# A gated delta-rule layer with a feed-forward block: a stated order of steps from the third chunk on, h W2 as seven products of blocks, K^T and Q^T in buffers of their own

## The chip, the cores and the metric

One core of one Trainium2 chip. The metric is the device time of one execution in microseconds (us); lower is better. TensorE (PE) multiplies, VectorE (DVE) and ScalarE (ACT) work elementwise, GpSimd (POOL) does some of that too, SyncE (SP) issues DMA transfers; ACT and POOL can issue them as well. Each engine works through a queue of its own in order, and waits in it for the results of others.

## The reference, cut to what matters

```python
# q, k, v: (4, 8, 768, 48), beta: (4, 8, 768); fp32
k_n = k / (norm(k) + 1e-6)
state = zeros(B, H, D, D)
for t in range(S):
    y[:, :, t] = einsum('bhd,bhde->bhe', q[:, :, t], state)
    v_old = einsum('bhde,bhd->bhe', state, k_n[:, :, t])
    state = state + beta_t * einsum('bhd,bhe->bhde', k_n[:, :, t], v_t - v_old)
x = y.transpose(0, 2, 1, 3).reshape(B, S, 384)
xn = (x - mean(x)) / sqrt(var(x) + 1e-6) * g_ln
out = x + maximum(xn @ w_ch1, 0) @ w_ch2      # w_ch1 384x1536, w_ch2 1536x384
```

## The kernel before, in words

The 768 tokens are cut into 12 chunks of C = 64 tokens, for all 4 batches at once: 256 rows of x a chunk. Two chunks make a slab. For a chunk the token loop is replaced by matrix work:

- **Loads.** `load_blocks` (L168) fetches K and Q in 32x32 blocks, K from chunk 4 on by POOL's queue, Q by SP's; `load_k` (L184) and `load` fetch K by rows and V, by SP.
- **K^T and Q^T.** `turned` (L348) transposes the blocks on DVE into the two halves of one tile `kqt` (three buffers).
- **Gram and product.** `gram` (L368) makes K K^T on PE, ACT copies it to `gsb` (L376, L383). `product` (L393) makes K Q^T, DVE masks it into `pt` (L395).
- **The inverse.** A triangular matrix of each chunk and head has to be inverted. `blocks(m)` does the 32x32 diagonal blocks for a slab (two chunks) on DVE: it clears the block `xb` (POOL, L535), transposes the gram (L477), scales it (L546), takes 31 elimination steps of two instructions each (L555, L560), and transposes the result (L483, `own`), which goes to `xt` (L468, L472). `join` (L574 to L631) then fills the blocks off the diagonal with small matmuls `p_e` (L580) and `p_z` (L626). `first_blocks` and `first_join` are a form with 16x16 blocks, for the first two slabs.
- **Scaling of v.** `norms` takes the norm of k: squares on ACT (L411, L413), sums on DVE (L417), root on ACT (L419), plus 1e-6 on POOL (L420). `scale_v` (L428) multiplies v by it, on POOL from chunk 2 on.
- **The recurrence.** `recur(c)`: `p_k` and `p_y` from K^T, Q^T and the state (L652), v minus `p_k` (L657), `p_u` (L663), `p_s` (L675) and the state's update (L678), `p_y` with `pt` (L683), its copy to x (L688), the layer norm (L694 to L701), and the transpose of its result `p_n` (L709) to `xnt` (L710).
- **The feed-forward block.** `ffn(c)`: 12 tiles of h, each 3 matmuls `p_h` in the program (L724; each is two instructions on PE, as are all 128-row fp32 products here but the transposes) and a relu on ACT (L730); then for each half of the rows 12 matmuls with w_ch2 into `p_o` (L746), the residual add on DVE (L735) and the store by SP (L737).

The order of the work: the first part is written out by hand under `in_this_order`, which ties the instructions of each engine to their written order. From chunk 0's feed-forward block on, a `Plan` gives every step a due time (T = 45 units a chunk); the steps are emitted by due time, and the scheduler may still move instructions between them. The recurrence of chunk c is due beside the feed-forward block of chunk c - 1, in some places beside its end; the grams and the inverse of the next slab are spread over the two chunks before it. `behind_each` keeps the joins behind the latest feed-forward matmul.

PSUM tiles have four tags: `att` (two buffers: p_e, p_z, p_n), `two` (one: p_g, p_k, p_u, p_s), `by` (one: p_y), `ffn` (two: p_h, p_o).

Of the kernel before, what the change touches and what calls it, by code (L numbers as in the profile page):

```python
# [67 lines left out]
@contextmanager  # L68
def behind(tc, last):

    with ExitStack() as stack:
        for ins in last.values():
            stack.enter_context(tc.issue_after(ins))
        yield


def behind_each(tc, last, gen):

    while True:
        with behind(tc, dict(last)):  # L80
            try:
                next(gen)
            except StopIteration:
                return
        yield
# [8 lines left out]
def kernel(  # L94
# [101 lines left out]

    def load_turned(c):
        load_blocks(k, c, 0, (nc.gpsimd,))
        load_blocks(q, c, 1, (nc.sync,))
# [146 lines left out]
    def turned(c, n):  # L346

        nc.vector.transpose(  # L348
            made[c][0][:, :, n].rearrange("p i (u t) -> p i u t", t=32), tblocks[(2 * c + n) % NTB]
        )  # L350

# [5 lines left out]
    def gram(c, fine=False, maker=ps_two):  # L357

        kqt = made[c][0]
        p_g = ps_g(maker)  # L360
        for j in range(GP):
            for u in range(2) if fine else (0,):
                for hp, e in TILES:
                    rows = slice(DP * hp, DP * hp + D)
                    i = e * GP + j
                    r0 = BK * u
                    out_ = p_g[C * e + r0 : C * e + r0 + (BK if fine else C), hp, j, 0 : C - r0]
                    nc.tensor.matmul(  # L368
                        out_, kqt[rows, i, 0, r0 : r0 + (BK if fine else C)], kqt[rows, i, 0, r0:C]
                    )  # L370
        dst = grams[c].rearrange("p (j n) t -> p n j t", n=2)
        if fine:
            nc.scalar.copy(dst[:, :, :, 0:BK], p_g[:, :, :, 0:BK])
            yield
        else:
            nc.scalar.copy(dst, p_g)  # L376
        for e in range(2):
            if fine:
                rows = slice(C * e, C * e + BK)
                nc.scalar.copy(dst[rows, :, :, BK:C], p_g[rows, :, :, BK:C])  # L380
            else:
                rows = slice(C * e + BK, C * e + C)
                nc.scalar.copy(dst[rows, :, :, 0:BK], p_g[rows, :, :, BK:C])  # L383

    def product(c):

        kqt = made[c][0]
        p_g = ps_g()
        for j in range(GP):
            for hp, e in TILES:  # L390
                rows = slice(DP * hp, DP * hp + D)
                i = e * GP + j
                nc.tensor.matmul(p_g[half(e ^ hp), hp, j], kqt[rows, i, 0], kqt[rows, i, 1])  # L393
        pt = work.tile([128, GH, C], FP32, name="pt", bufs=3)
        nc.vector.tensor_tensor(  # L395
            out=pt.rearrange("p (j n) t -> p n j t", n=2), in0=p_g,
            in1=pmask[:, None, None, :].to_broadcast([128, 2, GP, C]), op=ALU.mult,
        )
        made[c].append(pt)
# [4 lines left out]
    def norm_parts(c, scratch=None):  # L404
# [15 lines left out]
        nc.gpsimd.tensor_scalar_add(knrm, knrm, 1e-6)  # L420
# [6 lines left out]
    def scale_v(c, knrm, eng):  # L427
        eng.tensor_tensor(  # L428
            out=vs[c], in0=vs[c], in1=knrm[:, :, None].to_broadcast([128, GH, D]), op=ALU.mult
        )  # L430

    def new_chunk(c):
        if c % SLAB == 0:
            pairs[c // SLAB] = work.tile([128, SLAB, GH, C], FP32, name="gsb", bufs=2)
        grams[c] = pairs[c // SLAB][:, c % SLAB]
        made[c] = [work.tile([128, GH, 2, C], FP32, name="kqt", bufs=3)]

    def prep_v(c):
        if c > 2:
            load_kv(c)  # L440
        yield
        scale_v(c, norms(c), nc.gpsimd)
        yield

    def prep_g(c, fine=False):

        new_chunk(c)
        turned(c, 0)
# [5 lines left out]
    def prep_p(c):  # L454

        turned(c, 1)
# [5 lines left out]
    N_BLOCKS = 3 + BK // 2  # L462
# [11 lines left out]
    def blocks(m):  # L474
# [6 lines left out]
        def scatter(xb):  # L481
            own = blk.tile([128, SLAB * GH, BK], FP32, name="own", tag="gb")
            nc.vector.transpose(own.rearrange("p h t -> p t h"), xb[:, 0].rearrange("p s t -> p t s"))  # L483
            for i in range(SLAB):
# [39 lines left out]
    def inverse(nb, L, beta_l, gather, scatter):  # L524
# [10 lines left out]
        nc.gpsimd.memset(xb, 0.0)  # L535
        gb = square(both, 1) if L == FB else square(blk.tile([128, BK * BK], FP32, name="gb"), 0)
        gather(gb)
        yield
        nrm = blk.tile([128, BK], FP32, name="nrm")[:, 0 : nb * L].rearrange("p (b s) -> p b s", b=nb)
        nc.scalar.sqrt(nrm, diagonal(gb))  # L540
        nc.vector.tensor_scalar_add(nrm, nrm, 1e-6)
# [24 lines left out]
    N_JOIN = 2  # L566

    def join(chunks, both=()):

        last = None  # L570
        for c in chunks:
            xt, gsb = xts[c % NXT], grams.pop(c)
            xn = swapped("x_n").rearrange("p (h t) -> p h t", t=BK)
            nc.vector.transpose(xn, xt[:, :, 0:BK])  # L574
# [60 lines left out]
    N_RECUR = 6  # L635

    def recur(c):

        kqt, pt = made.pop(c)
        kp, xt, vv = kraws[c % NK], xts[c % NXT], vs[c]  # L640
# [5 lines left out]
        if c:  # L646
            p_k = ps(ps_two, "p_k")
            for n, dst in ((0, p_k), (1, p_y)):
                for j in range(GP):
                    for hp, e in TILES:  # L650
                        rows = slice(DP * hp, DP * hp + D)
                        nc.tensor.matmul(  # L652
                            dst[half(e), hp, j], kqt[rows, e * GP + j, n], s_all[rows, e, j],
# [43 lines left out]
        nc.scalar.activation(rstd, mv[:, :, 1], ACTF.Sqrt, bias=eps)  # L697
        nc.vector.reciprocal(rstd, rstd)
# [15 lines left out]
    N_FFN = FT + 2 * FT // 2  # L714

    mlp = {}

    def ffn(c):
        xnt, x = xnts.pop(c), xs.pop(c)
        hs = []  # L720
        for f in range(FT):
# [6 lines left out]
            mlp["PE"] = nc.cur_bb.bb.instructions[-1]  # L728
            h_f = work.tile([128, TOK], FP32, name="h_f", bufs=FT)
            nc.scalar.activation(h_f, p_h, ACTF.Relu)  # L730
            hs.append(h_f)
            yield
        def store(g, p_o):
            o = work.tile([128, DM], FP32, name="o", bufs=2)
            nc.vector.tensor_tensor(out=o, in0=p_o, in1=x[:, g], op=ALU.add)  # L735
            for e in range(2):
                nc.sync.dma_start(  # L737
                    out=out[2 * e + g, c * C : (c + 1) * C, :], in_=o[e * C : (e + 1) * C]
                )


        for gs in ((0, 1),) if c == 0 else ((0,), (1,)):
            p_os = [ps_ffn([128, DM], "p_o") for g in gs]
            for f in range(FT):
                for g, p_o in zip(gs, p_os):
                    nc.tensor.matmul(  # L746
                        p_o, hs[f][:, g * 128 : (g + 1) * 128], w2_sb[:, f],
                        start=(f == 0), stop=(f == FT - 1),
                    )
                mlp["PE"] = nc.cur_bb.bb.instructions[-1]  # L750
                if f % 2 and f < FT - 1:
                    yield
            for g, p_o in zip(gs, p_os):
                store(g, p_o)
            yield
# [9 lines left out]
    with in_this_order(tc) as last:  # L765
# [25 lines left out]
        scale_v(0, knrm, nc.vector)  # L791
# [5 lines left out]
        joining = join((0,), both=piece)  # L797
        next(joining)
# [22 lines left out]
        for _ in range(3):  # L821
# [6 lines left out]
    def second():  # L828
# [12 lines left out]
        scale_v(1, norms(1), nc.vector)  # L841
        yield

    def queries():
        for c in (2, 3):
            load_blocks(q, c, 1, (nc.sync,))
        load_kv(2)
        load_beta()

    T = 45  # L850
    starts = [0, 14, 64] + [80 + T * i for i in range(NCH - 2)]
    ends = [2, 26, 80] + starts[4:]
# [3 lines left out]

    plan.once(39, early.close)
    for c in range(NCH):
        t0, t1 = starts[c], ends[c]
        if c > 1:  # L860
            plan.spread(prep_v(c), 2, t0 - 72, t0 - 12)
        if c:
            plan.once(t0, begin, c)
        plan.spread(recur(c) if c else recur_0, N_RECUR if c else 1, t0, t1)
# [4 lines left out]
    plan.spread(ffn(1), N_FFN, 42, 80)  # L869
    for c in range(2, NCH):  # L870
        plan.spread(ffn(c), N_FFN, starts[c + 1], starts[c + 1] + T)
    for m in range(1, NSL):
        chunks = range(SLAB * m, SLAB * m + SLAB)
        t = starts[SLAB * m]
        if m > 1:

            times = (t - 70, t - 58, t - 18, t - 13) if m > 2 else (t - 56, t - 46, t - 18, t - 13)
            for i, c in enumerate(chunks):
                plan.once(times[0] - 15 + 5 * i, load_turned, c)
            plan.spread(in_turn(*(prep_g(c) for c in chunks)), SLAB * 2, times[0], times[1])  # L880
            plan.spread(blocks(m), N_BLOCKS, times[1], times[2])
            plan.spread(in_turn(*(prep_p(c) for c in chunks)), SLAB * 2, t - 25, t - 10)
        else:
            times = (16, 24, 44, 56)
            plan.spread(in_turn(*(prep_g(c, True) for c in chunks)), SLAB * 2, times[0], times[1])
            plan.spread(in_turn(*(prep_p(c) for c in chunks)), SLAB * 2, 30, 46)
            plan.once(10, queries)
            plan.spread(first_blocks(tuple(chunks)), 4 + FB // 2, times[1], times[2])

            def then(c):  # L890
                yield from first_join(c)
                to_xt(c)
                yield

            plan.spread(in_turn(*(then(c) for c in chunks)), 6, 44, times[3])
        joining = join(chunks)
        plan.spread(joining if m == 1 else behind_each(tc, mlp, joining), 3, times[3], t - 2)
    with behind(tc, after):
        plan.run()

# [29 lines left out]
```

## Time and profile before

| | |
|---|---|
| median of 4 runs | 617.01 us (609.12 to 619.4) |
| the profiled execution | 617.27 us, its span 615.4 us |
| PE busy | 541.2 us, 88% of the span |
| DVE busy | 322.6 us, 52% |
| ACT busy | 170.1 us, 28% |
| POOL busy | 80.5 us, 13% |
| granted TensorE clock, mean over the span | 0.971 |
| p_h matmuls (L724) | 206.7 us in 864 instructions |
| p_o matmuls (L746) | 201.5 us in 576 instructions |

The busy time of an engine is the time in which at least one of its instructions was at work; loads of weights into TensorE are counted apart (PEld) and run beside the matmuls. Matmuls overlap, so the mean duration of one is longer than the distance from one start to the next; the pace is read from starts in the timeline. A number in brackets in a timeline's line is the time that the engine had stood idle before it, and the instruction that ended that.

### The profile page before, as it was taken

The page shows a single profiled execution, that of the slowest core. Times are in us where ns is not written, and L with a number is a line of the kernel's source. Part 1 is how long each engine was busy: PE and PEld are TensorE (multiplying, and loading weights), DVE is VectorE, ACT ScalarE, POOL GpSimd, SP SyncE. Part 2 cuts the span into 40 slices and gives each one's busy share as a digit, 9 for nine tenths or more (in the row PEclk, how much of TensorE's full clock was granted, in tenths as well). Part 3 has the DMA queues.
Part 4 walks back from the last instruction along what each step waited for, and adds up shares of the span by engine and source line. Part 5 has one row for each costly group of instructions (what it writes and reads, how often), then busy time and mean ns, then how long its engine had stood idle before and what let it go on. Part 6 is the DMA issues. An engine that isn't in the chain of part 4 may idle for free.

```text
span 615.4 us, 20905 instructions
## 1 busy us (share of the span) xinstructions
PE 541.2 (88%) x9512; PEld 404.5 (66%) x9512; DVE 322.6 (52%) x681; ACT 170.1 (28%) x351; POOL 80.5 (13%) x128
## 2 busy tenths in 40 slices
PE   2036886987999959999999999999999999999997
PEld 2035665565767746866867867768758678677673
DVE  5835869993246993229964059952179720201000
ACT  1213252503333205241224232243322142122120
POOL 5000116331040202300302200011000010000000
PEclk9999879898999988999999999999999999999999
DMA  4716879526044600411610510200200000000101
GB/s 54 192 42 154 185 163 245 75 49 91 16 84 66 103 9 18 85 34 28 99 20 16 93 25 15 53 16 15 53 14 15 1 19 12 14 15 1 27 1 26
DMA packets 126919, 34.51 MB, mean 56 GB/s; under 512 B 121184, under 2 KB 124272, under 8 KB 126832
## 3 DMA queue, kind: packets, MB, share of 16 engines
q1 hardware_dynamic: 110256, 19.14, 18.8%
q0 software_dynamic: 3504, 10.25, 6.5%
q10 hardware_dynamic: 13072, 3.80, 2.7%
q8 instruction: 74, 1.21, 0.8%
q14 instruction: 13, 0.11, 0.1%
HBM read 28.44 MB, written 4.72 MB: 54 GB/s over the span
## 4 chain that ended last, share of the span: by engine, by line
PE 53%; DVE 27%; SPq 7%; issue 6%; DMA 3%; ACT 3%; ACTq 0%; DVEq 0%
PE p_o L746 20%; PE p_h L724 18%; DVE tmp L555 8%; DVE xb L560 8%; SPq L168 6%; PE p_g L368 2%; DMA tb<-in_k_dram 2%; PE p_e L580 2%; PE p_y L683 2%; PE p_z L626 2%; PE p_g L393 1%; DVE kqt L348 1%; DVE own L483 1%; SPq L184 1%; PE p_k L652 1%
## 5 line engine op out<-in xcount | busy, mean ns | idle before, releaser
L724 PE MATMUL p_h<-xnt,w_sb 128*128 128x256 f32 x864 | 206.7, 393 | 5.1 <-DVE o L735 4.4
L746 PE MATMUL p_o<-w_sb,h_f 128*128 128x384 f32 x576 | 201.5, 499 | 0.0
L724 PEld LDWEIGHTS p_h<-xnt,w_sb 128*128 128x128 f32 x864 | 164.4, 195 | 32.9 <-DVE o L735 4.0
L746 PEld LDWEIGHTS p_o<-w_sb,h_f 128*128 128x128 f32 x576 | 107.5, 193 | 65.8 <-issue 3.3
L730 ACT ACTIVATE h_f<-p_h 128x256 f32<-128x256 f32 x144 | 55.2, 383 | 192.6 <-PE p_h L724 192.5
L168 POOL DMA_DIRECT2D tb<-in_k_dram x64 | 42.5, 671 | 111.2 <-DVE tmp L555 57.4
L560 DVE TENSOR_TENSOR xb<-xb,tmp 128x31 f32<-128x31 f32 (+20 forms) x154 | 51.1, 332 | 5.1
L735 DVE TENSOR_TENSOR o<-p_o,x_ln 128x384 f32<-128x384 f32 x24 | 13.2, 549 | 74.0 <-PE p_o L746 74.0
L555 DVE TENSOR_TENSOR tmp<-xb,gb 128x31 f32<-128x31 f32 (+15 forms) x124 | 42.3, 341 | 3.8
L694 DVE BATCH_NORM_STATS2 st<-x_ln 128x6 f32<-128x384 f32 x24 | 12.3, 545 | 49.7 <-ACT x_ln L688 49.7
L678 DVE TENSOR_TENSOR s_all<-s_all,p_s 128x768 f32<-128x768 f32 x11 | 10.4, 941 | 47.2 <-PE p_s L675 47.1
L348 DVE STREAM_TRANSPOSE kqt<-tb 128x1024 f32<-128x1024 f32 x24 | 29.2, 1232 | 4.1 <-DMA tb<-in_k_dram 3.8
L368 PE MATMUL p_g<-kqt 48*64 48x64 f32 (+2 forms) x1024 | 16.9, 239 | 12.0 <-DVE kqt L348 8.1
L368 PEld LDWEIGHTS p_g<-kqt 48*32 48x32 f32 (+1 forms) x1024 | 14.8, 133 | 17.5 <-DVE kqt L348 8.3
L610 PE MATMUL p_e<-x_n,gsb 32*32 32x16 f32 x512 | 6.3, 189 | 22.4 <-DVE x_n L605 17.3
L420 POOL TENSOR_SCALAR knrm<-knrm 128x16 f32<-128x16 f32 x12 | 3.1, 256 | 163.9 <-ACT knrm L419 163.9
L417 DVE TENSOR_REDUCE ksum<-ksq 128x8 f32<-128x384 f32 x22 | 12.1, 550 | 21.2 <-ACT ksq L411 10.9
L580 PE MATMUL p_e<-x_n,gsb 32*32 32x32 f32 x768 | 16.1, 200 | 7.7 <-DVE mv L695 5.8
L580 PEld LDWEIGHTS p_e<-x_n,gsb 32*32 32x32 f32 x768 | 14.8, 113 | 11.0 <-DVE mv L695 6.0
L393 PEld LDWEIGHTS p_g<-kqt 48*64 48x64 f32 x768 | 14.0, 142 | 11.8 <-DVE s_all L678 6.5
L610 PEld LDWEIGHTS p_e<-x_n,gsb 32*32 32x32 f32 x512 | 5.7, 118 | 24.2 <-ACT xt L411 16.4
L657 DVE TENSOR_TENSOR v_raw<-v_raw,p_k 128x768 f32<-128x768 f32 x11 | 10.5, 952 | 20.8 <-PE p_k L652 20.8
(99 smaller groups left out, 521.1 us busy)
## 6 DMA issues: line engine op xcount, KB each, us to landing
words<-in_moe_w_ch_dram POOLq DMA_DIRECT2D x9, 768.0 KB, 5.6
out_dram<-o SPq DMA_DIRECT2D x48, 96.0 KB, 2.2
k<-in_k_dram SPq DMA_DIRECT2D x44, 96.0 KB, 3.1
v_raw<-in_v_dram SPq DMA_DIRECT2D x22, 192.0 KB, 4.3
tb<-in_q_dram SPq DMA_DIRECT2D x44, 64.0 KB
words<-in_moe_w_ch_dram ACTq DMA_DIRECT2D x3, 768.0 KB, 6.1
tb<-in_k_dram POOLq DMA_DIRECT2D x32, 64.0 KB, 2.8
tb<-in_q_dram SPq DMA_DIRECT2D x44, 32.0 KB, 2.2
```

What stands on the lines that cost most here:

```text
L168: engs[m % len(engs)].dma_start(out=dst[p0 : p0 + 32, :, u, 0:w], in_=src[:, hp::2, toks, 32 * m : 32 * m + w].rearrange("b j t d -> t (b ...
L348: nc.vector.transpose(made[c][0][:, :, n].rearrange("p i (u t) -> p i u t", t=32), tblocks[(2 * c + n) % NTB])
L368: nc.tensor.matmul(out_, kqt[rows, i, 0, r0 : r0 + (BK if fine else C)], kqt[rows, i, 0, r0:C])
L393: nc.tensor.matmul(p_g[half(e ^ hp), hp, j], kqt[rows, i, 0], kqt[rows, i, 1])
L555: nc.vector.tensor_tensor(out=t, in0=xb[:, :, 0:n, j : j + 1].to_broadcast([128, nb, n, w]), in1=gb[:, :, j : j + 1, j + 1 : L].to_broadca ...
L560: nc.vector.tensor_tensor(out=rest, in0=rest, in1=t, op=ALU.subtract)
L580: nc.tensor.matmul(p_e[r1, h], gsb[r0, h, BK:C], xn[r0, h])
L626: nc.tensor.matmul(p_z[r0, h], es[r1, h], xt[r1, h, BK:C])
L724: nc.tensor.matmul(p_h, w1_sb[:, t, f * 128 : (f + 1) * 128], xnt[:, t], start=(t == 0), stop=(t == KC - 1),)
L730: nc.scalar.activation(h_f, p_h, ACTF.Relu)
L735: nc.vector.tensor_tensor(out=o, in0=p_o, in1=x[:, g], op=ALU.add)
L746: nc.tensor.matmul(p_o, hs[f][:, g * 128 : (g + 1) * 128], w2_sb[:, f], start=(f == 0), stop=(f == FT - 1),)
```

## The change

**h W2 as seven products.** From chunk 1 on the product of h (256x1536) and w_ch2 (1536x384) is cut into 2x2 blocks: h into A11, A12, A21, A22 of 128x768, w_ch2 into blocks of 768x192. Instead of eight products of blocks there are seven, with sums of blocks (the Strassen-Winograd form): S1 to S4 are sums of blocks of h, made for each chunk on DVE (128x768 each; three of them in place); t2, t3, t4 are sums of blocks of w_ch2, made once on DVE (steps T), t1 takes the place of a block of w_ch2. P1 to P7 are the products, each six matmuls of 192 columns in the program, twelve instructions on PE. They add up in PSUM in three results, a, b and c; c and b are the two halves of one tile `p_o`. The steps d1 to d7 (eight instructions of 192 columns on DVE) read them and add them with x to the output.

**A stated order.** The plan ends with the joins of chunks 2 and 3. From chunk 2 on, `slot(c, order)` runs a string of steps, under `in_this_order` for all engines. A slot holds the recurrence of chunk c (KQ: L652 and v's subtraction; U; S; PU; L1 and L2: the layer norm; N: p_n), the feed-forward block of chunk c - 1 (H: one of twelve tiles of h with its relu; then S, P and d), the next chunks' transposes (TK, TQ), grams (G), products (PT, with the mask on DVE), and the inverse of the next slab (ga, no: gather and scale; r: two elimination steps; R: all that are left; own, xt, xn, J: the results and the joins). Vk and Vs: norms and scaling of v for chunk c + 1. An inverse is now done a slab ahead: its joins run in the odd slot before the slab that needs them. Slots 2 to 5 have strings of their own; slot 3 holds all elimination steps of the inverse for chunks 4 and 5.

**Smaller parts.** K^T and Q^T get tiles of their own (`kqt` becomes `kt` with 4 buffers and `qt` with 2). The loads for chunk c + 2 are issued right behind the transpose of chunk c, all by SP. Clearing `xb` goes from POOL to ACT for 32x32 blocks. The 1e-6 moves from POOL's L420 into `scale_v`, which is now always one DVE instruction. `load_kv(c + 2)` stands at the start of slot c; chunk 3's is fetched ahead of beta.

```diff
-        made[c] = [work.tile([128, GH, 2, C], FP32, name="kqt", bufs=3)]
+        made[c] = {}
...
+        made[c][n] = work.tile([128, GH, C], FP32, name="kq"[n] + "t", bufs=(4, 2)[n])
         nc.vector.transpose(
-            made[c][0][:, :, n].rearrange("p i (u t) -> p i u t", t=32), tblocks[(2 * c + n) % NTB]
+            made[c][n].rearrange("p i (u t) -> p i u t", t=32), tblocks[(2 * c + n) % NTB]
         )
+        if more and c + 2 < NCH:
+            load_blocks((k, q)[n], c + 2, n, (nc.sync,))
...
-        nc.gpsimd.tensor_scalar_add(knrm, knrm, 1e-6)
...
+        nc.vector.scalar_tensor_tensor(
+            out=vs[c], in0=knrm[:, :, None].to_broadcast([128, GH, D]), scalar=1e-6, in1=vs[c],
+            op0=ALU.add, op1=ALU.mult,
...
+            nc.scalar.mul(xb, eps[:, :, None, None].to_broadcast([128, nb, L, L]), 0.0)
...
+        t2, t3, t4 = (late.tile([128, HF, HM], FP32, name=f"t{i}") for i in (2, 3, 4))
+            for t, x0, x1 in ((t3, b22, b12), (b12, b12, b11), (t2, b22, b12), (t4, b21, t2)):
+                nc.vector.tensor_tensor(out=t, in0=x0, in1=x1, op=ALU.subtract)
+                yield
...
+    def mlp(c):
+        h, x = new_h(), xs.pop(c)
+        os = [work.tile([128, DM], FP32, name="o") for g in range(2)]
+        a11, a21, a12, a22 = (h[i][:, :, g * 128 : (g + 1) * 128] for i in range(2) for g in range(2))
+        s1, s2, s3, s4 = a21, a11, late_pool[0].tile([128, HF, 128], FP32, name="s3"), a12
...
+        def mul(n, a, b, first=False):
+            if n == "a" and first:
+                p["a"] = ps_ffn([128, HM], "p_a")
+            if n == "c" and "c" not in p:
+                p_cb = ps_ffn([128, DM], "p_o")
+                p.update(c=p_cb[:, 0:HM], b=p_cb[:, HM:])
+            for f in range(HF):
+                nc.tensor.matmul(
+                    p[n], a[:, f], b[:, f], start=(first and f == 0), stop=(f == HF - 1), skip_group_check=True,
+                )
...
+            "S3": lambda: add(s3, a11, a21, ALU.subtract),
+            "S1": lambda: add(s1, a21, a22),
+            "S2": lambda: add(s2, s1, a11, ALU.subtract),
+            "S4": lambda: add(s4, a12, s2, ALU.subtract),
+            "P1": lambda: mul("a", a11, w11, True),
+            "P2": lambda: mul("c", a12, w21, True),
+            "P5": lambda: mul("b", s1, t1),
+            "P6": lambda: mul("a", s2, t2),
+            "P3": lambda: mul("b", s4, w22),
+            "P7": lambda: mul("a", s3, t3),
+            "P4": lambda: mul("c", a22, t4, True),
+            "d1": lambda: add(o11, "a", x11),
+            "d2": lambda: add(o11, "c", o11),
+            "d5": lambda: add(o22, "b", x22),
+            "d6": lambda: add(o12, "a", x12),
+            "d3": lambda: (add(o12, "b", o12), store(c, 0, os[0])),
+            "d7": lambda: (add(o22, "a", o22), add(o21, "a", x21)),
+            "d4": lambda: (add(o21, "c", o21), store(c, 1, os[1])),
...
+    orders = {
+        2: """H H H KQ H H H T H T H T H T H U H S3 TK(a2) H P1 S1 d1 TK(b2) S2 S P2 d2 S4 PU P5 d5 L1
+            G(a2) P6 d6 L2 TQ(b) P3 d3 N G(b2) P7 d7 ga PT(b) P4 d4 no Vk Vs""",
+        3: """H r H KQ H r H r H r U TQ(a2) H r H r H r S H r PU H r H S3 H P1 S1 L1 d1 S2 PT(a2) L2
+            P2 d2 S4 r P5 d5 r P6 d6 TK(a4) N r P3 G(a4) d3 TK(b4) r P7 d7 G(b4) P4 d4 R own Vk Vs""",
+        4: """H H KQ xt' H xn' H H J' H H J' H U H J' H ga S H no S3 TQ(b) PU r H P1 L1 S1 PT(b) d1 S2
+            L2 P2 d2 S4 r P5 d5 r P6 d6 r N P3 d3 r P7 d7 r P4 d4 Vk Vs""",
+        5: """H r H KQ H r r H r H R U TQ(a2) H H own TK(a4) H S H H xt S3 PU H xn H L1 P1 S1 PT(a2) d1
+            S2 L2 P2 d2 S4 TK(b4) P5 d5 J P6 d6 G(a4) N P3 d3 J G(b4) P7 d7 J P4 d4 Vk Vs""",
+    }
+    even = """H H ga KQ no H r H r H r U H r H TQ(b) H r S H r H S3 PU r H H L1 P1 S1 PT(b) d1 S2 L2
+        P2 d2 S4 P5 d5 r P6 d6 r N P3 d3 r P7 d7 r P4 d4 Vk Vs"""
+    odd = """H r H r KQ H r H H R U TQ(a2) H H own TK(a4) H S H H xt S3 PU H xn H L1 P1 S1 PT(a2) d1 S2
+        L2 P2 d2 S4 TK(b4) P5 d5 J P6 d6 G(a4) N P3 d3 J G(b4) P7 d7 J P4 d4 Vk Vs"""
...
+    with in_this_order(tc):
+        for c in range(SLAB, NCH):
+            slot(c, orders.get(c, odd if c % SLAB else even))
+        steps = mlp(NCH - 1)
+        for name in "H H H H H H H H H S3 H H H P1 S1 d1 S2 P2 d2 S4 P5 d5 P6 d6 P3 d3 P7 d7 P4 d4".split():
+            steps[name]()
```

In the strings, a and b are the two chunks of the slot's slab, a2 and b2 those of the next, a4 and b4 of the one after; a prime marks a step for the slot's own slab.

## Prediction
> **What bounds the kernel now.** I read the page's first part, then its groups, then the table by stages, then the timeline.
>
> ```profile
> PE 541.2 (88%) x9512; PEld 404.5 (66%) x9512; DVE 322.6 (52%) x681; ACT 170.1 (28%) x351; POOL 80.5 (13%) x128
> L724 PE MATMUL p_h<-xnt,w_sb 128*128 128x256 f32 x864 | 206.7, 393 | 5.1 <-DVE o L735 4.4
> L746 PE MATMUL p_o<-w_sb,h_f 128*128 128x384 f32 x576 | 201.5, 499 | 0.0
> ```
> ```profile
> 247.00:334.00 87.00, 84.53 (x1404) 62.96 (x1404) 50.30 (x110) 26.35 (x55) 14.72 (x21) 1.00 0.27 47
> 334.00:421.00 87.00, 84.57 (x1404) 63.08 (x1404) 50.28 (x110) 26.35 (x55) 9.59 (x13) 1.00 0.20 38
> 421.00:508.00 87.00, 84.65 (x1406) 62.95 (x1404) 47.42 (x106) 24.68 (x51) 1.73 (x2) 1.00 0.09 20
> ```
>
> Columns of the second fence: window, length, busy time of PE, PE's weight loads, DVE, ACT and POOL (counts in brackets), then TensorE's clock, DMA share, GB/s. Each window is one pair of chunks. PE works 84.5 of 87 us at full clock; DVE 50. So from chunk 4 on TensorE is the bound, and only less TensorE work can gain much. The timeline says the same by start times:
>
> ```profile
> 246.88 1.15 PE L652 MATMUL p_k<-s_all,kqt 48*64 48x48 f32 x64
> ...
> 286.88 1.56 PE L724 MATMUL p_h<-xnt,w_sb 128*128 128x256 f32 x6 [0.93 <-DVE o L735]
> 288.37 1.15 PE L652 MATMUL p_k<-s_all,kqt 48*64 48x48 f32 x64
> ...
> 309.99 1.16 PE L393 MATMUL p_g<-kqt 48*64 48x64 f32 x64 [1.26 <-DVE s_all L678]
> ```
> ```profile
> 229.05 1.92 PE L580 MATMUL p_e<-x_n,gsb 32*32 32x32 f32 x64 [5.82 <-DVE mv L695]
> ```
>
> The next pair begins at 334.12, so a pair takes 87.24 us. The waits in brackets are all that PE loses in steady state; the 5.82 us (a join behind the inverse, once, for chunks 4 and 5) is the largest after 165 us.
>
> **Durations that I use.** From starts on PE:
>
> ```profile
> 281.26 0.82 PE L709 MATMUL p_n<-ident,xn_ln 128*128 128x128 f32 x6
> 281.91 2.75 PE L746 MATMUL p_o<-w_sb,h_f 128*128 128x384 f32 x8
> ...
> 571.93 7.91 PE L746 MATMUL p_o<-w_sb,h_f 128*128 128x384 f32 x24
> 579.67 15.70 PE L724 MATMUL p_h<-xnt,w_sb 128*128 128x256 f32 x72
> 595.21 15.64 PE L746 MATMUL p_o<-w_sb,h_f 128*128 128x384 f32 x48
> ```
>
> p_o: 24 in 7.74 us, 322.5 ns for 384 columns. p_h: 72 in 15.54, 215.8 ns for 256. The line through both is 2.5 ns + 0.833 ns a column. p_n: 6 in 0.65, 108 ns for 128 (line: 109).
>
> **The seven products.** h W2 is 48 instructions of 384 columns a chunk, 15.48 us. After, it is 7 x 6 x 2 = 84 of 192 columns. 192 columns do not occur before. Low end: the line, 162.5 ns, 13.65 us. High end: the weight load sets the pace, and the load groups of p_h and p_o show 195 and 193 ns, so 195 ns, 16.38 us. I take the line: p_n's load lasts 147 ns in its group, yet its matmuls start every 108, so a load's recorded length is not the time by which it holds the next matmul. That is -1.83 us a chunk, for 11 chunks (chunk 0 keeps the plain form) -20.1 us; at the high end +9.9.
>
> The Trainium skill ("TensorE: Matmul & The Clock Gate", section "Back-to-back issue gap") speaks against this edit: in a stream of weight load and matmul pairs the spacing is set by both, 81 ns at 128 columns where the column count alone gives 56. An estimate by that page, 25 ns more on each of 924 matmuls, would be +23 us, about 625 instead of the forecast below. The p_n row above shows no such excess at 128 columns, so the sum does without it.
>
> **What the products cost DVE.** By the rows 128x384 (0.549) and 128x1024 (L546, 1.23), 192 columns are 0.35 us and 768 are 0.95. A chunk gains S1 to S4 (3.8), eight output adds (2.8), loses two L735 (1.1), and takes v's scaling from POOL (L428, 1.475 there; 0.96 on DVE, as in its two early calls): +6.5. A pair goes from 50.3 to 63.3 us, under PE's 78 to 81. The four weight sums (1152 columns, 1.36 each) run once, in chunk 2's slot. On average all of it is hidden; in order it isn't, see below.
>
> **Moved and hidden.** K^T's eight loads a chunk go from POOL's queue to SP's, behind chunk c's transpose and ahead of later stores: 8 x 0.6 us (two L168 issue in 1.14) more in a queue that then issues for about 18 us in a 40 us slot, one or two slots early; uncovered, 5 us a slot. Clearing the inverse's block goes from POOL to ACT, a 128x1024 pass, 1.0 us by L376; ACT is busy 26 of 87 us; uncovered, 5 in all. POOL's knrm add goes; DVE waited for it only 8.0 us, early. Own buffers for K^T and Q^T remove a dependence on old products, worth nothing while loads are early. The inverse one chunk ahead removes the 5.82 us, which the sum below drops by construction.
>
> **The start, T0.** Before, the last join of chunks 2 and 3 ends on PE at 165.1, with all twelve H steps (one H is six p_h matmuls, 1.3 us) of chunk 1's FFN among them. After, that FFN belongs to slot 2, and only its first three H and KQ (chunk 2's products with the state, 2.0) can move up. 165.1 - 15.5 + 3.9 + 2.0 = 155.5; PE's idle gaps there (1.67, 1.09, 1.41, 1.00) take about 3.5 of these: T0 = 152. Bounds: 148 (all fits in gaps) and 157 (DVE's inverse sets it).
>
> **The slots, in PE work.** H 15.54 + products 13.65 + KQ 2.01 + U, S and PU 3.24 + p_n 0.65 + PT 1.09 = 36.2. Odd slots add two grams (2.2) and the joins (3.5): 41.9. With each order's own steps: slot 2 (36.2, with two grams, without KQ and three H) 32.5; slot 3 (with two grams) 38.4; 4 (with the joins that slot 3 has no room for) 39.7; 5 and 7 41.9; 6, 8 and 10 36.2; 9 (joins, no grams left) 39.7; 11 (no S, no PT) 34.0; the last FFN (15.54 + 13.65) 29.2: together 405.9. Changes between big and small tiles cost 0.1 to 0.2 each, 0.8 to 1.6 a slot, 11.7 in all.
>
> **New waits.** Two results, c and b, share one tile p_o. P5 writes b, so it waits for d2, DVE's read of c after P2. Between P1 and d2 DVE's order holds PT's mask, d1, S2, L2: pt 1.14, d1 0.28, S2 0.87, L2 1.07, d2 0.35, 3.7 us against P2's 1.95. So PE stands about 1.9 us in each slot from 3 on; behind P5 stand P6, P3, P7, P4 and the next slot, so this is not made up. Slots 6, 8: 2.1; 7, 9: 2.5 with a wait for the copy of p_n; 10: 1.9; 2, 11 and the end 0.8 in all. In slot 3 the whole inverse for chunks 4 and 5 runs: DVE has 43 to 45 us, PE 39.4, and the lag goes on: 3.3 in slot 3, 5.5 in slot 4 (its join waits about 2 for DVE, P5 3.2), 7.8 in slot 5, where R puts five steps (6.9 us) and own, TK, xt ahead of d2. Together 28.5. DVE's neighbours overlap by some 5% (transposes of 1.23 start 1.16 apart), so I take 2.4 off: 26.1. Bounds: 0 and about 45 (slots 6 to 10 as slot 5).
>
> **Sum.** 152 + 405.9 + 11.7 + 26.1 + 4.5 (after PE's last matmul, as before) = 600.2 span; 1.9 lies around it (617.27 against 615.4): 602.1, 2.5% under that execution, which is 0.26 above the median 617.01 of runs between 609 and 619. A measurement here tells about 2%: below 604.7 is faster, above 629.4 slower.
>
> **Rivals.**
> 1. DVE keeps up: P5 hardly waits, and slots 3 to 5 cost little. For it: DVE has 63 us in 81. Against: its queue is in order, and L2 and pt stand before d2. 602 - 26 = 576 with no stall; likely 586, 574 to 592.
> 2. DVE's lag doesn't drain: after slot 5, each slot starts late on DVE, relus wait behind knrm on ACT, and PE waits in H as well as at P5. For it: nothing in an even slot is left empty on DVE until the inverse's steps end. Against: 63 of 81. Stalls of 45 instead of 26: 621; with T0 157 and some unhidden SP issues up to 632.
> 3. The slower side: the weight load sets the pace at 192 columns. For it: loads of 193 to 195 ns in both groups. Against: the p_n row. The place is P1 to P7; the price 924 x (load - 162.5 ns): at 190 ns 25.4, 627; at 195 ns 30.0, 632. It decides from 192 ns on, where the sum passes 629.4.
>
> **Chances.** Forecast (592 to 612) 0.50, of it 0.30 below 604.7; rival 1 0.20; rival 2 0.18, of it 0.05 slower; rival 3 0.12, of it 0.09 slower. So faster 0.30 + 0.20 = 0.50; slower 0.05 + 0.09 = 0.14; the same 0.36. The predicted time is the forecast's 602. Its own range is 592 to 612; for 8 in 10 I add most of rival 1 and half of rival 2: 580 to 624.
>
> **What would show it.** Right: p_a, p_o, p_b matmuls of 192 columns starting every 162 to 163 ns; per slot one PE gap at P5 of 1.5 to 2.5 us, put down to DVE, and larger ones in slots 4 and 5; a pair of chunks at about 85 us from chunk 6 on against 87.24; KQ of chunk 2 done near 152. Wrong: 190 ns spacing (rival 3); pairs near 81 (rival 1); DVE without idle time after slot 5 or long waits of H for ACT (rival 2); a T0 outside 148 to 157, or waits on SP's transfers, which I left at nothing.

## The result, and the profile after

The changed kernel takes 619.25 us (median of 43 runs, 614.29 to 624.88); the kernel before 615.9 (median of 64, one of them an outlier of 2667 us). The ratio is 1.0064, 95% interval [1.005, 1.0079]: a little slower, and 17 us above the 602 that were forecast; it lies outside the forecast's own range (592 to 612) and inside the wider one (580 to 624). The profiled execution took 622.23 us, 3 us over the median; its span is 620.2 us, against 600.2 in the sum.

First the page's busy times, then the new groups:

```profile
PE 535.4 (86%) x9908; PEld 468.1 (75%) x9908; DVE 388.0 (63%) x805; ACT 172.0 (28%) x355; POOL 16.2 (3%) x38
...
L781 PE MATMUL p_o<-w_sb,h 128*128 128x192 f32 x396 | 73.8, 338 | 18.8 <-DVE o L786 18.8
...
L781 PE MATMUL p_a<-t,h 128*128 128x192 f32 x132 | 25.3, 344 | 0.0
```

PE's busy time fell by only 6 us where 20 had been taken away, and DVE gained 65. The 18.8 us of idle time ahead of p_o are P5 waiting for d2. The pace, from starts in the timeline of the last block:

```profile
608.12 2.11 PE L781 MATMUL p_a<-t,h 128*128 128x192 f32 x12
610.07 2.11 PE L781 MATMUL p_o<-w_sb,h 128*128 128x192 f32 x12
```

Twelve matmuls of 192 columns in 1.95 us: 162.5 ns each, the value on the line. So work did go; where did the time come back? The ends of the slots (the end of P4, from PE's timeline), beside the forecast's terms:

| part | forecast us | measured us | of that at half clock |
|---|---|---|---|
| T0 | 152 | 158.6 | 128.5 to 132.0, 138.7 to 158.6 |
| slot 2 | 33.7 | 36.0 | 158.6 to 162.7 |
| slot 3 | 42.9 | 41.5 | none |
| slot 4 | 46.6 | 48.2 | 244.6 to 248.1 |
| slot 5 | 51.3 | 58.8 | 316.2 to 326.6, 336.7 to 340.2 |
| slot 6 | 39.1 | 39.0 | none |
| slots 7 to 11 and the last block | 232.5 | 233.7 | none |

(A slot's forecast is its PE work, its waits, and 0.8 to 1.6 us for the changes between big and small tiles; the forecast then took 2.4 off for overlap on DVE.) From slot 6 on the walk holds: even slots 39.0 against 39.1, the odd one 46.5 against 46.0. Nearly all of the loss is in the start and in slots 4 and 5, and there stands what the forecast left out: TensorE's granted clock. Windows of the changed kernel (columns as in the prediction's second fence; the clock is the number ahead of the last two):

```profile
313.50:316.90 3.40, 0.00 (x0) 0.00 (x0) 3.36 (x8) 0.00 (x0) 0.00 (x0) 0.91 0.11 11
316.90:320.30 3.40, 3.11 (x10) 3.11 (x11) 2.25 (x3) 0.00 (x0) 0.00 (x0) 0.50 0.02 4
320.30:323.70 3.40, 3.40 (x70) 2.90 (x69) 0.36 (x1) 0.41 (x1) 0.00 (x0) 0.50 0.72 95
323.70:327.10 3.40, 3.40 (x20) 3.17 (x22) 0.04 (x1) 0.77 (x2) 0.00 (x0) 0.58 0.20 22
327.10:330.50 3.40, 3.40 (x81) 3.33 (x79) 0.32 (x1) 2.25 (x4) 0.00 (x0) 1.00 0.00 0
```

PE stands still for one window, and then works for nearly 10 us at half clock. The timeline shows the same stretch; the two DVE lines are the inverse's last transpose, and d2, for which P5 waits:

```profile
303.89 2.09 DVE L463 STREAM_TRANSPOSE own<-xb 128x1024 f32<-128x1024 f32 x1
...
316.78 0.35 DVE L786 TENSOR_TENSOR o<-p_o,o 128x192 f32<-128x192 f32 x1
317.19 4.21 PE L781 MATMUL p_o<-w_sb,h 128*128 128x192 f32 x12 [5.89 <-DVE o L786]
321.33 1.92 PE L564 MATMUL p_e<-x_n,gsb 32*32 32x32 f32 x64
323.18 3.85 PE L781 MATMUL p_a<-t,h 128*128 128x192 f32 x12
```

Twelve matmuls take 4.1 and 3.8 us instead of 1.95. The wait itself (5.89 us) is shorter than the 7.8 us that the forecast had for slot 5; the half clock behind it was not in the sum. The 3.4 us from 336.7 on follow a second gap, of 2.20 us, ahead of a gram: the profile names nothing that PE waited for there, and the queue that loads instructions moves a packet just before, so it is taken for a fetch of instructions. The profile of before has half clock too, behind its own long wait of 5.82 us:

```profile
223.20:229.00 5.80, 0.03 (x4) 0.00 (x0) 5.73 (x13) 0.00 (x0) 0.95 (x1) 0.63 0.01 3
229.00:235.00 6.00, 5.95 (x71) 4.07 (x72) 4.25 (x9) 3.04 (x6) 0.00 (x0) 0.51 0.19 38
```

In all, the records of before show half clock for 34 us up to its last matmul, those of after for 58.

Every run lists its span s and mean clock c. Since the clock in these records is 1 or 0.5, 2(1-c)s is the time at half clock, shown in the table below; it includes time in which PE has nothing to do. Runs more than 1.5% above the fastest of the same kernel are left out of the ratios and of these half clock times, but not of the medians.

### The profile page after: what moved, and what is told of

It is laid out like the page before. It is cut to its first block, busy times and chain, and to the rows that moved or that the text cites. A ratio compares the mean times of both kernels' runs of the same rounds, so it can differ in the third digit from the quotient of the medians.

```text
span 620.2 us, 21738 instructions
## 1 busy us (share of the span) xinstructions
PE 535.4 (86%) x9908; PEld 468.1 (75%) x9908; DVE 388.0 (63%) x805; ACT 172.0 (28%) x355; POOL 16.2 (3%) x38
## 3 DMA queue, kind: packets, MB, share of 16 engines
q8 instruction: 77, 1.26, 0.8%
## 4 chain that ended last, share of the span: by engine, by line
PE 65%; DVE 21%; issue 7%; DMA 3%; ACT 3%; SPq 0%; POOL 0%; ACTq 0%; DVEq 0%; POOLq 0%
PE p_h L728 26%; PE p_o L781 11%; PE p_a L781 10%; DVE xb L544 4%; DVE tmp L539 4%; PE p_e L564 2%; PE p_z L610 2%; PE p_g L356 2%; PE p_u L647 2%; DVE h L786 2%; PE p_s L659 2%; PE p_y L667 1%; PE p_k L636 1%; PE p_g L381 1%; DVE o L786 1%
## 5 line engine op out<-in xcount | busy, mean ns | idle before, releaser
L732 ACT ACTIVATE h<-p_h 128x256 f32<-128x256 f32 x144 | 54.8, 382 | 158.3 <-PE p_h L728 151.4
L781 PE MATMUL p_o<-w_sb,h 128*128 128x192 f32 x396 | 73.8, 338 | 18.8 <-DVE o L786 18.8
L781 PEld LDWEIGHTS p_o<-w_sb,h 128*128 128x128 f32 x396 | 65.5, 194 | 22.4 <-DVE o L786 21.7
L786 DVE TENSOR_TENSOR h<-h 128x768 f32<-128x768 f32 x33 | 31.3, 949 | 17.8 <-ACT h L732 17.7
L356 PE MATMUL p_g<-kt 48*64 48x64 f32 (+2 forms) x1024 | 17.2, 242 | 14.0 <-DVE kt L334 8.3
L781 PE MATMUL p_a<-t,s 128*128 128x192 f32 x132 | 25.6, 345 | 0.2 <-issue 0.2
L781 PE MATMUL p_a<-t,h 128*128 128x192 f32 x132 | 25.3, 344 | 0.0
L577 ACT ACTIVATE es<-p_e 32x512 f32<-32x512 f32 x23 | 13.5, 588 | 40.4 <-PE p_e L564 37.0
L786 DVE TENSOR_TENSOR o<-p_a,x_ln 128x192 f32<-128x192 f32 x33 | 11.6, 351 | 19.5 <-PE p_a L781 19.5
L781 PE MATMUL p_o<-t,h 128*128 128x192 f32 x132 | 23.8, 330 | 0.0
L781 PEld LDWEIGHTS p_a<-t,s 128*128 128x128 f32 x132 | 22.8, 199 | 0.8 <-issue 0.5
L781 PEld LDWEIGHTS p_a<-t,h 128*128 128x128 f32 x132 | 23.2, 202 | 0.3
```

The costliest lines, as they stand in the source:

```text
L356: nc.tensor.matmul(out_, kt[rows, i, r0 : r0 + (BK if fine else C)], kt[rows, i, r0:C])
L577: nc.scalar.mul(es[r1], p_e[r1], -1.0)
L732: nc.scalar.activation(h[f // HF][:, f % HF], p_h, ACTF.Relu)
L781: nc.tensor.matmul(p[n], a[:, f], b[:, f], start=(first and f == 0), stop=(f == HF - 1), skip_group_check=True,)
L786: nc.vector.tensor_tensor(out=out_, in0=p[in0] if isinstance(in0, str) else in0, in1=in1, op=op)
```

## The experiments

All against the kernel before on the same chip (its median there is 615.4 to 615.8 us).

| kernel | runs | median us | ratio to before, 95% | median half clock us |
|---|---|---|---|---|
| before | 25 | 615.8 | | 29.5 |
| changed | 43 | 619.25 | 1.0064 [1.005, 1.0079] | 54.6 |
| changed, again | 12 | 619.88 | 1.0072 [1.0044, 1.0101] | 49.4 |
| H steps back beside the inverse | 10 | 613.86 | 0.996 [0.9919, 1.0001] | 34.8 |
| filler in the start | 6 | 624.78 | 1.0131 [1.0086, 1.0176] | 32.1 |
| slot 5 anew | 10 | 614.67 | 0.9999 [0.9972, 1.0026] | 47.8 |
| filler in slot 5 | 10 | 619.64 | 1.0031 [0.9995, 1.0066] | 51.5 |
| fillers in slots 4 and 5 | 12 | 613.52 | 0.9968 [0.9935, 1.0002] | 38.6 |
| d2 first | 4 | 605.78 | 0.983 [0.9782, 0.9878] | 56.0 |
| order without products | 9 | 620.65 | 1.0079 [1.0044, 1.0113] | 48.4 |
| products without order | 6 | 631.23 | 1.0241 [1.0198, 1.0284] | 55.4 |
| all mends | 6 | 592.84 | 0.9645 [0.9598, 0.9691] | 24.1 |
| all mends, no products | 6 | 610.37 | 0.9888 [0.9831, 0.9944] | 20.7 |

**H steps back beside the inverse.**

```diff
+    plan.once(41, first_mlp)               # mlp(1) and sum_blocks()
+    plan.spread(first_hs(), FT, 42, 61)    # the twelve H steps of chunk 1
-        2: """H H H KQ H H H T H T H T H T H U H S3 TK(a2) H P1 S1 d1 TK(b2) S2 S P2 d2 S4 PU P5 ...
+        2: """KQ S3 P1 S1 d1 T T U S2 P2 d2 S4 TK(a2) S T T P5 d5 PU TK(b2) G(a2) L1 P6 d6 ...
```

> The twelve H steps of chunk 1's feed-forward block go back beside the inverse and joins of chunks 2 and 3, where they stood before the change; slot 2 starts with KQ and mixes its products with the recurrence. Theory (TensorE's granted clock falls to half where PE is thinly used, and the 24 us at half clock from 139 to 163 us are the missed cost): half clock there at most 7 us, P4 of slot 2 ends at 186 to 188 us instead of 194.6, total 610 to 613 us. Rival (the start is set by DVE's inverse and the joins; the H steps only change places): P4 of slot 2 still ends near 194, total 617 to 621.

KQ of chunk 3 starts at 185.1 us instead of 197.3, so slot 2 ends near 182.4. In its profile the clock is full from 113.5 to 260 us. The median is 5.4 us lower (6.4 by the ratios), the half clock 20 us less. That is the theory's direction, and at the edge of its size (610 to 613); its profiled execution, 604.8 us of span, is its shortest. The run moves real work and raises the clock at once; the next one was to part the two.

**Filler in the start.**

```diff
+        p_f = ps_ffn([128, TOK], "p_f")
+        for _ in range(3):
+            nc.tensor.matmul(p_f, w1_sb[:, 0, 0:128], w1_sb[:, 1, 0:TOK], start=True, stop=True)
+    for t in (44.5, 46.5, ..., 60.5):
+        plan.once(t, fill)
```

> The changed kernel with 27 added products of 256 columns (54 instructions, 11.6 us at full clock) between the joins of chunks 2 and 3, whose result nobody reads; the H steps stay in slot 2. It tells the clock from the moved work. Theory (the half clock from 139 to 163 us comes from PE's thin use): with more work PE keeps its clock, and slot 2 ends no later than 194.6 us although 11.6 us of work are added; total 614 to 620, half clock there under 10 us. Rival (the clock does not matter there): the filler is paid for, 625 to 631.

Between the two, and nearer the rival: 11.6 us of useless work cost 5.5 us, and half clock fell by 22 us in the median. In the profile slot 2 ends at 199.5 us (194.6 in the changed kernel), and the half clock between 128 and 163 us is 13.7 us instead of 27.3, not under 10. About 6 us came back. The clock need not be the reason for all of it: PE's waits in that stretch are 7.6 and 8.6 us in the two profiles of the changed kernel and 3.8 here, so some 4 us of the filler ran in time in which PE had stood idle, at no cost whatever the clock. How much the clock costs in the start is not shown by this run.

**Slot 5 anew.**

```diff
-        5: """... H R U TQ(a2) H H own TK(a4) H S H H xt S3 PU H xn H L1 P1 S1 PT(a2) d1 S2 L2 P2 d2 S4 TK(b4) P5 d5 J ...
+        5: """... H R U H H H S H H S3 PU H L1 H P1 S1 d1 S2 P2 d2 S4 P5 d5 L2 own TQ(a2)
+            P6 d6 N TK(a4) P3 xt d3 PT(a2) xn P7 d7 G(a4) TK(b4) P4 J d4 G(b4) J Vk Vs""",
+        6: """H H J' ga KQ no ...
```

> Slot 5 alone is ordered anew: d2 stands on DVE ahead of own, TK, TQ, xt and PT's mask, and the last join step moves into slot 6. Theory (stall plus half clock after it): the 5.9 us wait at P5 goes, and with it the 13.6 us at half clock that follow: about -6 -6, total 605 to 609 us, no half clock from 310 to 345 us. Rival 1 (only the stall counts, the clock is harmless): -6, 613. Rival 2 (DVE's work is only put off, the joins wait in its place): 617 to 621.

From KQ to KQ, slot 5 fell from 58.8 to 46.9 us and its 13.6 us at half clock went. Slot 6 rose from 39.0 to 42.4: the join put off into it, a gap of 1.43 us without a releaser and 3.4 us at half clock behind that. Small waits came up at P5, PT and the grams (0.45, 0.58, 0.82). The median gained 4.6 us of the 12 that the theory expected. A second profile of the changed kernel (below) has slot 5 at 54.3 us; against that one, 7.4 us went in slot 5 and 3.4 came back in slot 6. So the stall and its half clock went, as the theory has it, but part of the gain was only put off, as rival 2 has it.

**Filler in slot 5.** "F" in slot 5's string runs 17 added products between P2 and d2.

```diff
-            S2 L2 P2 d2 S4 TK(b4) P5
+            S2 L2 P2 F d2 S4 TK(b4) P5
```

> 17 added products of 192 columns (34 instructions, 5.5 us at 162.5 ns) whose result nobody reads are run between P2 and P5 of slot 5, where PE otherwise waits 5.9 us for DVE. No wait of the kernel is changed. Theory (the clock falls because PE idles): the wait itself stays covered by the filler, P6, the joins and P7 behind it run at full clock, 5 to 7 us less, total 612 to 614.5, no half clock from 317 to 341 us. Rival (the clock falls for another reason, such as the small tiles of the joins, or costs nothing): 618 to 621.

The timed runs say the rival's number. The profile says that slot 5 fell from 58.8 to 50.4 us without half clock; but in it an instruction fetch of 2.07 us, which had stood in slot 5 (2.20), now stood in slot 7, with a window at half clock behind it. With one slot's effect the medians can't tell. So it was run again, with more of the same, beside the changed kernel:

> The changed kernel once more, as the partner of the next run and for a second look at slots 4 and 5. Both theories: 617 to 621 us. If the half clock in slot 5 belongs to its 5.9 us wait, this profile has it again (some 10 us at half clock within 12 us of that wait, slot 5 from KQ to KQ 55 to 59 us); if it was chance, slot 5 is near 52.

```diff
-        4: """H H KQ xt' H ... L2 P2 d2 S4
+        4: """H H KQ F6 xt' H ... L2 P2 F8 d2 S4
-        5: """... L2 P2 d2 S4
+        5: """... L2 P2 F17 d2 S4
```

> Filler products whose result nobody reads in all three long waits of slots 4 and 5: 12 instructions behind KQ of slot 4, 16 ahead of P5 of slot 4, 34 ahead of P5 of slot 5 (192 columns each, 10.1 us of added work in waits of 2.25, 2.69 and 5.89 us). Theory (a wait costs its length and then half of the half clock that it brings): no half clock from 240 to 345 us, 20 us of it less, 5 to 9 us less than the changed kernel in the same call. Rival (the clock's loss is made up elsewhere): within 2 us of it.

The changed kernel again had half clock right behind its 5.89 us wait, slot 5 at 54.3 us (6.8 us at half clock behind the wait where the first profile has 10.2, and none behind the fetch, 1.80 us here: the length differs from run to run). With 10.1 us of work more, the kernel is 6.4 us faster than its partner, and the intervals of the two ratios don't touch. In the two profiles slots 4 and 5 became 3.4 and 3.9 us shorter and slot 7 0.7 longer; about 1 us of that is a shorter fetch. The timeline of the filler kernel and its windows:

```profile
309.38 5.69 PE L966 MATMUL p_f<-w_sb 128*128 128x192 f32 x34
315.44 2.22 PE L781 MATMUL p_o<-w_sb,h 128*128 128x192 f32 x12 [0.36 <-DVE o L786]
317.58 1.20 PE L564 MATMUL p_e<-x_n,gsb 32*32 32x32 f32 x64
```
```profile
238.00:247.00 9.00, 8.88 (x162) 7.61 (x161) 8.41 (x17) 1.66 (x6) 0.00 (x0) 1.00 0.72 132
...
310.00:345.00 35.00, 34.43 (x714) 31.11 (x713) 21.26 (x47) 15.08 (x28) 0.00 (x0) 1.00 0.33 55
```

The same matmuls behind the wait now run at full clock (changed kernel, same windows: 0.87 and 0.80 in its first profile, 0.84 and 0.90 in its second). Nothing but useless work was added; this shows that an idle PE costs more than its idle time here.

**d2 first.**

```diff
-    even = """... L1 P1 S1 PT(b) d1 S2 L2 P2 d2 S4 P5 d5 r P6 ...
+    even = """... L1 P1 S1 d1 S2 P2 d2 S4 PT(b) P5 L2 d5 r P6 ...
```

The same move in the strings of slots 3, 4, 5 and the odd slots.

> In slots 3 to 11 PT moves between P2 and P5 and L2 behind P5, so that d2 is the first thing DVE does after S2. Theory (P5 waits for d2 because c and b share a tile): the waits at P5 of 1.26, 2.69 and five times 1.57 go, in slot 5 some 2 of 5.9: 11 to 14 us less, total 605 to 608. Rival (the wait moves on to P3, which needs d5, or to p_n, which needs L2): gaps of 1 to 1.5 us there, total 615 to 619.

As the theory said, 13.5 us less (four runs). In the steady slots the wait is gone and none took its place: even slots 37.2 us instead of 39.0, odd 44.9 instead of 46.5. Slot 5 keeps 4.23 of its 5.89 us, as expected. The changed kernel has this wait in each slot from 6 to 10, behind PT's mask and L2 on DVE:

```profile
407.07 1.23 DVE L383 TENSOR_TENSOR pt<-p_g,pmask 128x1024 f32<-128x1024 f32 x1 [1.70 <-PE p_g L381]
...
409.53 0.87 DVE L686 TENSOR_SCALAR xn_ln<-x_ln,mv,rstd 128x384 f32<-128x384 f32 x2
410.31 0.35 DVE L786 TENSOR_TENSOR o<-p_o,o 128x192 f32<-128x192 f32 x1
410.72 2.22 PE L781 MATMUL p_o<-w_sb,h 128*128 128x192 f32 x12 [1.57 <-DVE o L786]
```

and the kernel with d2 first has PT's product in that place, without a bracket (from the kernel with all mends, where the strings are the same):

```profile
384.92 2.11 PE L781 MATMUL p_o<-w_sb,h 128*128 128x192 f32 x12
386.96 1.16 PE L381 MATMUL p_g<-qt,kt 48*64 48x64 f32 x64
388.05 2.22 PE L781 MATMUL p_o<-w_sb,h 128*128 128x192 f32 x12
```

**The order without the products.** The strings stay; P1 to P7 stand for parts of the plain product, S, T and most d for nothing.

```diff
+            "P1": lambda: mul(0, range(0, 4)), "P2": lambda: mul(0, range(4, 8)), "P5": lambda: mul(0, range(8, 12)),
+            "P6": lambda: mul(1, range(0, 3)), ...   # 384 columns, rows g = 0 or 1
+            "d5": lambda: end(0), "d4": lambda: end(1),
```

> The stated order is kept, but h W2 is computed as before, 48 instructions of 384 columns a chunk in the places of P1 to P7; the sums S, T and six of the eight output adds are gone. This tells the products' price from the order's. Theory (products save 1.83 us a chunk on PE, but their sums delay d2 and P5): PE +20.1, the waits at P5 (11.8 and 5.9 us) and the weight sums gone, DVE 5.5 us a slot lighter: the same within 8 us of the changed kernel, 612 to 626, no gap ahead of p_o. Rival (the products cost nothing, only the start and slot 5 do): 634 to 640.

620.65, within a microsecond or two of the changed kernel. An even slot takes 39.0 to 39.5 us, with the products 39.0: in the changed kernel the wait of 1.57 us at P5 ate the 1.83 us that the products save. So the stated order, with the smaller parts but without the products, is 0.8% slower than the plan before, and in that order the products changed nothing that these runs can tell.

**The products without the order.** In the kernel before, from chunk 2 on:

```diff
+        for names in ("S3 P1 S1", "d1 S2", "P2 d2 S4", "P5", "d5", "P6", "d6", "P3", "d3", "P7 d7", "P4", "d4"):
+            for n in names.split():
+                steps[n]()
+            yield
```

> The kernel before with its plan and its order; only h W2 becomes seven products from chunk 2 on, with S, d and the weight sums placed by due times. This is the products without the stated order. Theory (the products pay 1.83 us a chunk where DVE has room): 10 chunks, -18, with some waits for d2: 600 to 608. Rival (PE waits for DVE's sums wherever they are put, as in the changed kernel): 614 to 622.

Slower by 2.4%, beyond both expectations. Its profiled execution is the longest of its runs, so only its waits are read. DVE works at the inverse ahead of S2 and d2, so PE waits, and half clock follows (6.8 to 10.2 us per pair of chunks in its records from chunk 4 on):

```profile
322.82 0.94 DVE L808 TENSOR_TENSOR h<-h 128x768 f32<-128x768 f32 x1
...
323.82 2.29 PE L802 MATMUL p_a<-t,h 128*128 128x192 f32 x6 [4.83 <-DVE h L808]
```

**All mends.** H steps beside the inverse, d2 first, slot 5 anew, and in slot 3 this:

```diff
-  ... P7 d7 G(b4) P4 d4 R own Vk Vs
+  ... P7 d7 G(b4) P4 d4 Vk Vs R own
```

> All mends at once: the H steps of chunk 1 beside the first inverse, d2 ahead of PT's mask and L2 in all slots, slot 5 ordered anew, and in slot 3 the scaling of v ahead of the last elimination steps, so that slot 4's relus don't wait for the norm. Theory (the three costs are separate, measured alone at about -6, -13 and -4.5, with 2 for slot 4): 590 to 597 us, half clock under 30 us in all. Rival (they share the same loss, since each stall only matters by the half clock that follows): 600 to 606.

592.84 us: 0.9645 of the kernel before, [0.9598, 0.9691], and 26 us under the changed one. The gains alone were 5.4, 13.5 and 4.6; they add up, with some 3 us left; slot 3's edit was not run alone. The edit in slot 3 took the wait of H (2.25) and left one of 2.71 at the join in its place. This is the fastest version run here.

**All mends, without the products.**

> The mended kernel (all mends at once, 592.8 us) with h W2 computed as before the change, 48 instructions of 384 columns. Theory (seven products are worth their 1.83 us a chunk on PE once nothing waits for d2): 11 x 1.83 = 20 us more, 610 to 615. Rival (DVE's lighter work gives part of it back): 600 to 608.

17.5 us more than with them by the medians and 15 by the ratios, of the 20 that the columns alone give. An even slot takes 39.0 us without the products and 37.2 with them, the 1.83 us of the sum. Here the products earn their place; the line is from the mended kernel with products:

```profile
L781 PE MATMUL p_o<-w_sb,h 128*128 128x192 f32 x396 | 71.0, 329 | 2.1 <-DVE o L786 2.1
```

Its idle time ahead of p_o is 2.1 us in place of 18.8.

## Why the prediction was wrong, point by point

- **What bounds the kernel** (TensorE, from chunk 4 on): right. Where a mend took a wait of PE away (d2 first), the slots became shorter by at least its length (1.8 us for 1.57 in an even slot). From slot 6 on a pair of chunks takes 85.6 us, as forecast, against 87.24 before: there the change gains.
- **162.5 ns for 192 columns, rival 3 refused:** right. The loads of these groups still read 190 to 202 ns in the mean, and don't set the pace. By the Trainium skill ("TensorE: Matmul & The Clock Gate", section "Back-to-back issue gap") load and matmul set the spacing together; the prediction's estimate from it was 25 ns more a matmul. The trace shows no such excess: 162.5 ns, as on the line.
- **P5 waits for d2, 1.9 us a slot:** right in place, 1.57 us in size (its own terms, 3.71 less 1.95, give 1.76); d2 first shows what it is worth with the waits of slots 3 to 5, 13.5 us. It was in the sum. The prediction set it beside a gain of 1.83 us a chunk, and didn't say that the two are equal: without the wait the same products pay 15 to 17.5 us, with it nothing.
- **Slots 3 to 5, 3.3, 5.5 and 7.8 us of waits:** they came where they were walked, and shorter: 1.26, 4.94 (2.69 at P5 for 3.2, and 2.25 in H where 2 at the join were expected) and 5.89. What failed is the price: a wait was put at its own length, the clock behind it at nothing. In the profile 13.6 us at half clock belong to the waits of slots 4 and 5, and 3.4 more follow the fetch of 2.20 us in slot 5, which was not in the sum either: some 8 us of lost work. The fillers gave 6.4 back.
- **T0 = 152:** the step that failed most. It measured 158.6, outside its bounds of 148 to 157, and slot 2 took 2.3 more. The prediction counted the H steps taken out as PE time saved, and didn't ask what they had covered. Without them PE has waits and small tiles there, and the clock is at half from 138.7 to 162.7 us. All seven profiles with the changed start and no filler in it have 24 to 31 us at half clock there, the three of kernels with the H steps put back 0 to 3.4. Put back, they gave 5.4 us; the filler in their place gave about 6 against its own price, some 4 of them by filling idle time.
- **"The inverse one chunk ahead removes the 5.82 us":** it did, with the 10.2 us at half clock that came with it before, and put a 5.89 us wait with as much into slot 5. So nothing was won there.
- **The overlap of 2.4 us on DVE:** it can't be told apart. PE's waits for DVE and ACT from slot 3 on come to 21.4 us, under the 26.1 of the sum and the 28.5 without the overlap.
- **Rival 2 (621 us):** its number is near the measured one, its mechanism didn't come: from slot 6 on DVE is busy for 61.5 of 85.6 us a pair, the waits at P5 stay at 1.57 us, and PE waits for no relu in H.
- **SP's transfers, left at nothing:** right; from slot 2 on neither PE nor DVE is seen to wait for a transfer.

The sum of the misses, from the table: T0 6.6, slot 2 2.3, slot 3 -1.4, slot 4 1.6, slot 5 7.5, slot 6 -0.1, the rest 1.2, overlap 2.4, behind the last matmul -0.2: 19.9 of the 20.0 between 600.2 and the span 620.2. By cause, as an estimate from these rows: 8.9 in the start and slot 2, some 8 of half clock in slots 4 and 5, 2.2 for the fetch, -4.7 for waits put too high; the 5 to 6 left are in the slots' PE work.

What stays open: how much of T0's loss is the clock and how much the cover itself; the two runs give 5.4 and about 6 and don't part them. And the length of the half clock behind one and the same wait differs between executions (10.2 and 6.8 us behind the 5.89 us in slot 5), so its price could not have been given ahead to better than a few us.

## What to carry to other kernels

Where TensorE is the bound, price a wait of some microseconds (2.25 to 5.89 here) at its length plus half of the time that the clock then stays down, and look at the granted clock of before at its own long wait for a size. When a change takes matmuls away from a stretch of small or late work, ask what they kept busy, not only what they cost. Of two results that share one PSUM tile, the read of the first is part of the path of the second: put that read ahead of everything else on its engine, and give PE an unrelated product to run meanwhile.

## What the runs showed of the hardware

Busy is not enough to bring the clock back. In the start of the changed kernel PE had matmuls in nearly all of these windows, and the clock stayed at half:

```profile
146.10:149.50 3.40, 3.12 (x69) 2.40 (x73) 0.53 (x1) 1.07 (x2) 0.00 (x0) 0.50 0.02 5
149.50:153.00 3.50, 3.50 (x154) 3.35 (x154) 0.00 (x0) 0.48 (x2) 0.00 (x0) 0.50 0.02 5
153.00:156.40 3.40, 3.25 (x106) 2.98 (x104) 2.12 (x3) 1.75 (x3) 0.00 (x0) 0.50 0.02 5
156.40:159.80 3.40, 3.40 (x77) 3.06 (x72) 3.37 (x4) 0.58 (x1) 0.00 (x0) 0.50 0.02 5
159.80:163.20 3.40, 3.40 (x10) 2.72 (x10) 1.98 (x2) 0.38 (x1) 0.00 (x0) 0.58 0.00 0
163.20:166.60 3.40, 3.40 (x18) 2.99 (x17) 1.41 (x2) 1.15 (x3) 0.00 (x0) 1.00 0.00 0
```

Up to 158.6 us most of that work is in tiles of 32x32 and 48x64; from then on it is p_h in 128x128, and 4 us later the clock is full. With the H steps mixed into the same joins it stays full (the windows 139.3 to 149.5 and 149.5 to 159.8 of that kernel: 1.00, PE busy 9.57 of 10.20 and 10.09 of 10.30 us). The wait at P5 of slot 5 points the same way. Two windows behind it, in the first profile of the changed kernel and then in the second:

```profile
319.65:323.10 3.45, 3.45 (x70) 3.01 (x68) 0.36 (x1) 0.00 (x0) 0.00 (x0) 0.50 0.61 80
323.10:326.50 3.40, 3.40 (x16) 3.34 (x13) 0.00 (x0) 1.18 (x2) 0.00 (x0) 0.50 0.32 39
```
```profile
319.10:322.55 3.45, 3.45 (x12) 3.40 (x11) 1.66 (x2) 0.00 (x0) 0.00 (x0) 0.50 0.17 23
322.55:325.95 3.40, 3.40 (x78) 3.01 (x76) 0.36 (x1) 1.18 (x2) 0.00 (x0) 1.00 0.67 86
```

PE is busy throughout. The first profile's window up to 323.10 is half P5 and half a join in 32x32, and the clock stays down for one window more, which is nearly all P6 in 128x128; the second's up to 322.55 is P5 alone, and the clock is full behind it. That is the difference between 10.2 and 6.8 us. So it seems to be the use of the array, not the presence of matmuls, that counts; no run here took the tile size alone.

Nor did PE have to stand still for 3.4 us: from 241.20 to 244.60 it had matmuls for 1.41 of 3.40 us (the wait of 2.25 us in slot 4), and the clock went to half for the next 3.4.

The Trainium skill ("TensorE: Matmul & The Clock Gate", section "Part 1: The HAM clock gate (the "warmup" mystery)") gives half clock after an idle window of some 3.4 us and full clock after a busy one. The lengths at half clock in the traces are multiples of 3.4 us, as such windows would give (3.4, 6.8, 10.2, 23.9). The windows above that are busy by the profile and still at half, and the half clock behind the wait of 2.25 us, this rule does not foresee.
